# Spectral mixing and softmax attention on one core: the planner counts loaded matrix entries as usable later

## Chip, cores and metric

The kernel runs on one core of one Trainium2 chip. The metric is the device time of one execution in microseconds (us); lower is better. TensorE (PE) does the matrix products, ScalarE (ACT) the exponentials and copies, VectorE (DVE) and GpSimd (POOL) elementwise work, SyncE (SP) issues most of the transfers.

## Reference

Two branches over different inputs x [1, 2048, 448]; their results stand side by side in an output [1, 2048, 896].

```python
# A: spectral mixing, y = Re(DFT_seq(DFT_hidden(x))), with the DFT matrices given as inputs
a = einsum("bsd,ed->bse", x, dft_hid_re)
b = einsum("bsd,ed->bse", x, dft_hid_im)
y = einsum("ts,bse->bte", dft_seq_re, a) - einsum("ts,bse->bte", dft_seq_im, b)
# B: attention with 16 heads of 28
q, k, v = split((x @ wqkv))                 # wqkv [448, 3 * 448]
p = softmax(q @ k.T * 28 ** -0.5)           # 2048 x 2048 for each head
out = (p @ v) @ wo
concatenate([y, out], axis=-1)
```

The two sequence matrices are 2048 x 2048 f32, 16 MB each.

## The kernel before

**What is computed where.** The attention goes head by head. For one head, TensorE makes the scores of 16 key tiles by 4 query chunks of 512 (L1280), ScalarE takes their exponentials (L1286), and TensorE multiplies them by the values (L1263). Ahead of each head its first key tile is treated apart to get the shift of the exponentials: scores (L1221), a copy by ScalarE (L1225), transposes and maxima on VectorE (L1226 to L1247), a cast of the shift row into the queries (L1250), a subtraction from the first tile's scores (L1252, "the shift"; on VectorE or GpSimd), and the exponentials of this tile (L1254). A head ends with ScalarE's copy of the output bank (L1312), a reciprocal on VectorE (L1314 to L1320), a product on GpSimd (L1323) and stores to an intermediate tensor (L1329).

**The filling.** TensorE's remaining time goes to the projections (L684) and to the spectral branch (L864), which is stored through L1091, L1092, L1093 (sum and difference halves), L1117 and L1119 (output rows) and the transfers L1124 (GpSimd) and L1131 (SP). Behind the attention stands the output projection: loads of its operand (L1399, L1406, L1410), a split in high and low parts (L1424 on ScalarE, L454 elsewhere) and matmuls (L1444).

**The matrix check.** The sequence matrices are used in folded form. Beside the attention the kernel loads their entries into six raw buffers of 512 KB (`raw_s`, NRAW = 6) and looks at whether they have the symmetry that the folding takes for granted: differences and sums of two buffers (L950, on GpSimd 2.3 or VectorE 1.2 us in the plan) and the largest absolute value (L896, `far`). Most loads go through SP in ascending row order (L915). Entries that must be read in descending order (class `Turned`) go through GpSimd's own queue: four pieces of 128 KB (L938), and for some of them two edge loads (L943), which wait for all four pieces.

**What sets the order.** Nothing is ordered by hand. Each instruction is a task with a key (its due time, in planned us), the engines that may take it with a planned duration, and the tasks that it needs. `Schedule.run` plays the plan through: an idle engine takes the ready task with the smallest key, and a task becomes ready when its inputs count as there. The order in which the plan took them is the order in which each engine's queue is written; on the chip every engine works its queue strictly in that order. So a planned duration that is wrong makes no error, it only puts instructions in another order.

When a load through SP counts as usable is

```python
landed.append(max(at + 1.35 + size / 170 + extra + ..., flow + 1.1))   # size in KB
lat = max(landed[-len(t.dmas):]) - at + 0.1 + t.slack
```

with `slack = SLACK` on the loads of matrix entries, of the projection pieces and of the input rows. A load through GpSimd (`far_dma`) counts as usable a fixed number of us after its issue.

The due times of the attention are spread evenly from T_ATT to T_END, `P_H = (T_END - T_ATT) / H` for each head; those of the filling follow the points of PACE, of which the last is (all work, T_FILL). T_OUT belongs to the output projection.

Of the kernel before, what the change touches and what calls it, by code (L numbers as in the profile page):

```python
# [33 lines left out]
NKEPT = 16  # L34
NKEYS = 4
NFILL = 1
SLACK = 3.0
FILL_AT = 48.0, 75.0
N_WARM = 9
N_FIRST = 3  # L40
# [310 lines left out]
def tile_kernel(ctx, tc, xa, wre, wim, wd, xb, wqkv, wo, out):  # L351
# [53 lines left out]
    class Half:  # L405


        def __init__(self, pair, i):
            self.pair, self.i = pair, i
# [24 lines left out]
    def dma(key, emit, size=256, extra=0.0, n=1, **kw):  # L434

        return sch.add({"SP": 0.4}, key, lambda e: emit(), dmas=[(size, extra)] * n, **kw)

    def far_dma(key, emit, lat, d=1.2, **kw):

        return sch.add({"POOL": d}, key, lambda e: emit(), lat=lat, **kw)  # L440

    def act(key, emit, d=ACT_P, **kw):
        return sch.add({"ACT": d}, key, lambda e: emit(), **kw)
# [4 lines left out]
    def pool(key, emit, d=POOL_2, **kw):  # L448
        return sch.add({"POOL": d}, key, lambda e: emit(), **kw)
# [16 lines left out]
            nc.vector.tensor_copy(dst, src)  # L466


    T_ATT, T_END, T_FILL, T_OUT = 50.0, 620.0, 660.0, 630.0
    P_H = (T_END - T_ATT) / H  # L470
    begins = [T_ATT + h * P_H for h in range(H)]
    dt = P_H / (NT * NC)
# [9 lines left out]
    def fkey(n, d):  # L482

        f = clock[0]
        clock[0] += n * d
        for (f0, t0), (f1, t1) in zip(PACE, PACE[1:]):
            if f < f1 or f1 == F_TOTAL:
                return t0 + (f - f0) * (t1 - t0) / (f1 - f0)
# [87 lines left out]
    def load_folded(part, key, after):  # L576
# [3 lines left out]
        cols = slice(part * D, (part + 1) * D)  # L580
        lw = [dma(key, lambda: nc.sync.dma_start(w()[:, :, :E], wd[:, :2, part * D:part * D + E]), 226, slack=SLACK, use=[raws[2]])]
        ld = dma(key + 0.5, lambda: nc.sync.dma_start(n()[:, :, :D], wd[:, :2, cols]), 448, acq=[raws[0]])
        ld2 = dma(key + 0.7, lambda: nc.sync.dma_start(n2()[:, :, :D], wd[:, 2:, cols]), 448, acq=[raws[1]])
        ld3 = [dma(key + 1, lambda: nc.sync.dma_start(r()[:, :, :E], wt_d[:, :, part * D:part * D + E]), 226, slack=SLACK, deps=turned[0], use=[raws[3]])]
        f = lambda l: w_first.folded[:, part, :, l, :]
# [17 lines left out]
    class Piece:  # L603


        def __init__(self, src, key):
            self.hi, self.lo = whi.slot(), wlo.slot()
            raw = Square(raw_s.slot())
            ld = dma(key, lambda: nc.sync.dma_start(raw.t, src()), 256, slack=SLACK, acq=[raw])
            a = act(key + 1, lambda: nc.scalar.activation(self.hi.t, raw.t, AF.Copy), ACT_S, soon=SOON,  # L610
# [189 lines left out]
    def tokens(c, key, after):  # L800
# [6 lines left out]
        for q, st in enumerate((c, NH - 1 - c)):  # L807
            ln.append(dma(key + 0.3 * q, lambda q=q, st=st: nc.sync.dma_start(
                n.t[:, q].rearrange("p (b x) -> p b x", b=2), bass.AP(tensor=xa.tensor, offset=xa.offset + st * tile_x,
                ap=[[4 * P, P], [NH * tile_x, 2], [1, 2 * P]])), 256, slack=SLACK, use=[n]))  # L810
            lr.append(dma(key + 0.3 * q + 0.1, lambda q=q, st=st: nc.sync.dma_start(
                r.t[:, q].rearrange("p (b x) -> p b x", b=2), bass.AP(tensor=xt_d.tensor, offset=xt_d.offset + st * tile_x // 2,
                ap=[[2 * P, P], [NH * tile_x // 2, 2], [1, 2 * P]])), 256, slack=SLACK, deps=turned[1], use=[r]))
        z = [pool(key, lambda p=p, k=k: nc.gpsimd.memset(r.t.rearrange("p a (b k m) -> p (a b) k m", b=2, k=2)[p:p + 1, :, k], 0.0), 0.3, deps=lr, use=[r])
# [84 lines left out]
    row_n, tile_n = NT * P, P * NT * P  # L899
# [3 lines left out]
    def begun(key):  # L903
        return [opened[min(max(int((key - begins[0]) / P_H), 0), H - 1)]]

    class Stack:
# [6 lines left out]
        def loads(self, part, key, n, off, step):  # L913
            src, rows = (wre, wim)[part], P // n
            return [dma(key, lambda a=a: nc.sync.dma_start(self.t[a * rows:(a + 1) * rows], bass.AP(  # L915
                tensor=src.tensor, offset=src.offset + off(a), ap=[[step, rows], [1, H1]])), 512 / n, slack=SLACK, deps=begun(key), use=[self.raw]) for a in range(n)]

# [14 lines left out]
    class Turned(Stack):  # L932


        def __init__(self, part, b, key):
            self.raw = raw = raw_s.slot()
            src = (wre, wim)[part]
            at = lambda rows, cols, off, ap: far_dma(key, lambda: nc.gpsimd.dma_start(self.t[rows, cols], bass.AP(  # L938
                tensor=src.tensor, offset=src.offset + off, ap=[[tile_n, 4], *ap, [1, cols.stop - cols.start]])), 5.0 + SLACK, d=0.7, deps=begun(key), use=[raw])
            q = H1 // 4  # L940
            self.ld = [at(slice(0, P), slice(i * q, (i + 1) * q), H1 + i * q + (P - 32 * b) * row_n, [[-row_n, 32]]) for i in range(4)]
            if not b:
                at = lambda cols, off: far_dma(key, lambda: nc.gpsimd.dma_start(self.t[0:P:32, cols], bass.AP(  # L943
                    tensor=src.tensor, offset=src.offset + off, ap=[[tile_n, 4], [1, cols.stop - cols.start]])), 3.0 + SLACK, d=0.6, deps=self.ld[:4], use=[raw])
                self.ld += [at(slice(0, H1 - P), H1 + P), at(slice(H1 - P, H1), 0)]
# [409 lines left out]
    key = fkey(0, 0)  # L1355
# [35 lines left out]
    for n, c in enumerate(range(NC)):  # L1391
        raws = []
        for k in range(4):
            pair = kept_s.slot()
            raw = Half(pair, 0)
            key = T_OUT + n
            deps = [o_done[h, c] for h in range(H - 1) if (h + 1) * DH > k * P and h * DH < (k + 1) * P] + [before["k"] if n > 1 else opened[H - 1], *starts[max(4 * n - 8, 0):max(4 * n - 7, 0)]]
            if k < 3:
                ld = dma(key, lambda raw=raw, k=k, c=c: nc.sync.dma_start(raw.t, on_d[k * P:(k + 1) * P, c * CH:(c + 1) * CH]),  # L1399
                         deps=deps, use=[pair])  # L1400
# [13 lines left out]
        for i in range(2):  # L1414
            x = [Flat(p.slot()) for p in (whi, whi, wlo, wlo)] if i else [q_s.slot() for _ in range(4)]
            ready = [[], []]
            for k in range(4):
                raw, ld = raws[k]
                src = lambda raw=raw, i=i: raw.t[:, i * HF:(i + 1) * HF]
# [3 lines left out]
                key = T_OUT + T_CONV + n + i / 2  # L1423
# [3 lines left out]
                else:  # L1427
                    b = sub(key, lambda hi=hi: hi()[64:], lambda src=src: src()[64:], lambda hi=hi: f32(hi())[64:], d=0.35, early=True,
                            deps=[a], use=[raw.pair, xh, xl])
                ready[k // 3] += [a, b]  # L1430
            for t in range(2):
# [7 lines left out]
                key = T_OUT + O_AT + (n * 4 + i * 2 + t) * 2.3 + (100 if final else 0)  # L1439

                def emit(e, seq=seq, o=o, at=0, to=9):
                    for n, (x, w) in enumerate(seq):
                        if at <= n < to:
# [8 lines left out]
                             deps=[m], use=[o, pair]) for way, c0, c1 in ways]  # L1452
# [157 lines left out]
```

## Time and profile before

| what | value |
|---|---|
| time, median of 3 runs | 761.42 us (760.31 to 763.87) |
| profiled execution | 760.66 us, its span 759.1 us |
| TensorE busy | 719.0 us (95%), granted clock 0.979 |
| ScalarE busy | 610.1 us (80%) |
| VectorE busy | 532.7 us (70%) |
| GpSimd busy | 368.3 us (49%) |
| bytes moved | 127.80 MB, mean 168 GB/s |

The busy times are of one execution. Waits stand beside them in brackets: the idle time of an engine just before an instruction, and what ended it. The granted clock of TensorE is a share of its full speed, as a mean over the stretch asked for. From about 60 to 704 us the sixteen heads run one behind another; the copies L1312 mark their ends (the first at 108.00, the last at 704.34).

### The profile page before, as it was taken

To read this page: it belongs to the slowest core of one execution; us is meant where nothing else is said; L and a number is where in the kernel's file an instruction comes from. 1 tells how busy PE (TensorE), PEld (TensorE's weight loads), DVE (VectorE), ACT (ScalarE), POOL (GpSimd) and SP (SyncE) were. 2 spreads that over 40 slices of the span, in tenths; PEclk is the share of its full clock that TensorE was granted. 3 is DMA by queue.
4 is the path that set the end of the run, shared out by engine and by line. 5 is a ranking of instruction groups with operands and counts; after the bars stand their busy time and mean duration, and the time that the engine had idled before them with its cause. 6 is when DMAs were issued, how large, how long until landed. Compare 5 with 4: busy or idle time off the path is not lost. (4 is left out here: it accounts for less than half of the span.)

```text
span 759.1 us, 12950 instructions
## 1 busy us (share of the span) xinstructions
PE 719.0 (95%) x4147; PEld 402.8 (53%) x4147; DVE 532.7 (70%) x872; ACT 610.1 (80%) x1232; POOL 368.3 (49%) x357
## 2 busy tenths in 40 slices
PE   8899999989999997999799999899999999999877
PEld 7697444545545453454334454445445554555766
DVE  5558539767777889686687688987989846522752
ACT  6316899878989988899687999888989899999142
POOL 7202425655262656572545447555787433436640
PEclk9999999999999999999889999999999999999989
DMA  8657539674859989967678397657161413331466
GB/s 307 221 175 219 137 85 239 166 200 120 219 151 214 259 200 250 223 181 177 166 197 222 105 247 191 184 169 231 53 183 58 118 33 82 93 87 53 111 185 223
DMA packets 116160, 127.80 MB, mean 168 GB/s; under 512 B 54470, under 2 KB 80728, under 8 KB 116084
## 3 DMA queue, kind: packets, MB, share of 16 engines
q1 hardware_dynamic: 109300, 120.75, 58.2%
q0 software_dynamic: 6784, 6.14, 3.4%
q8 instruction: 35, 0.57, 0.3%
q14 instruction: 41, 0.34, 0.2%
HBM read 96.64 MB, written 32.69 MB: 170 GB/s over the span
## 5 line engine op out<-in xcount | busy, mean ns | idle before, releaser
L1286 ACT ACTIVATE kept<-bank 128x512 f32<-128x512 f32 x960 | 499.2, 687 | 38.8 <-PE bank L1280 36.9
L1280 PE MATMUL bank<-q,k 98*128 98x512 f32 x960 | 316.1, 423 | 17.5 <-ACT kept L1286 10.7
L1280 PEld LDWEIGHTS bank<-q,k 98*128 98x128 f32 x960 | 172.9, 190 | 173.7 <-issue 92.4
L1263 PE MATMUL bank<-kept,v 128*32 128x512 f32 x2048 | 248.9, 607 | 0.5 <-ACT kept L1286 0.5
L950 POOL TENSOR_TENSOR raw<-raw,raw 128x1024 f32<-128x1024 f32 (+3 forms) x60 | 119.9, 2003 | 107.4 <-DMA raw<-wre 55.2
L1263 PEld LDWEIGHTS bank<-kept,v 128*32 128x32 f32 x2048 | 55.8, 110 | 121.2 <-issue 114.2
L896 DVE TENSOR_REDUCE far<-raw 128x1 f32<-128x1024 f32 (+2 forms) x78 | 86.2, 1111 | 17.1 <-POOL raw L950 10.7
L1226 DVE STREAM_TRANSPOSE mb<-bank 128x512 f32<-128x512 f32 x64 | 45.3, 710 | 48.2 <-PE bank L1221 44.4
L1250 POOL CAST q<-mb 1x512 fp32r<-1x512 f32 x32 | 27.7, 870 | 67.5 <-DVE mb L1247 61.8
L1254 ACT ACTIVATE kept<-kept 128x512 f32<-128x512 f32 x64 | 46.8, 749 | 15.9 <-DVE kept L1252 11.4
L1225 ACT ACTIVATE kept<-bank 128x512 f32<-128x512 f32 x64 | 40.5, 673 | 22.4 <-PE bank L1221 18.6
L684 PE MATMUL bank<-big,whi 128*128 128x512 f32 x132 | 50.2, 409 | 7.1 <-DVE kept L707 4.4
L1323 POOL TENSOR_TENSOR kept<-kept 128x512 f32<-128x512 f32 x16 | 20.6, 1285 | 67.2 <-DVE kept L1318 36.6
L1252 POOL TENSOR_TENSOR kept<-kept,mb 128x512 f32<-128x512 f32 x32 | 43.6, 1368 | 11.1 <-DVE mb L1247 8.3
L1227 DVE TENSOR_REDUCE qm<-mb 128x16 f32<-128x512 f32 x64 | 43.3, 679 | 1.4
L1247 DVE STREAM_TRANSPOSE mb<-am 128x512 f32<-128x512 f32 x64 | 43.2, 695 | 0.8
L684 PE MATMUL bank<-wd,big 128*128 128x224 f32 x288 | 43.7, 278 | 0.0
L684 PEld LDWEIGHTS bank<-wd,big 128*128 128x128 f32 x288 | 40.5, 195 | 5.2 <-issue 2.5
L1314 DVE STREAM_TRANSPOSE kept<-kept 128x512 f32<-128x512 f32 x16 | 11.3, 708 | 39.3 <-ACT kept L1312 39.3
L1252 DVE TENSOR_TENSOR kept<-kept,mb 128x512 f32<-128x512 f32 x32 | 35.3, 1107 | 0.5
L950 DVE TENSOR_TENSOR raw<-raw,raw 128x1024 f32<-128x1024 f32 (+3 forms) x24 | 34.1, 1420 | 1.9 <-DMA raw<-wre 1.8
L1250 DVE CAST q<-mb 1x512 fp32r<-1x512 f32 x32 | 34.1, 1079 | 0.8
(174 smaller groups left out, 819.7 us busy)
## 6 DMA issues: line engine op xcount, KB each, us to landing
raw<-wre SPq DMA_DIRECT2D x64, 256.0 KB
raw<-wim SPq DMA_DIRECT2D x64, 256.0 KB
qkd<-kept SPq DMA_DIRECT2D x40, 256.0 KB
k<-qkd SPq DMA_DIRECT2D x64, 112.0 KB
q<-qkd SPq DMA_DIRECT2D x64, 112.0 KB
kept<-xb SPq DMA_DIRECT2D x16, 256.0 KB
vd<-kept SPq DMA_DIRECT2D x32, 128.0 KB
v<-vd SPq DMA_DIRECT2D x16, 256.0 KB
```

Source lines behind the costliest of these rows:

```text
L684: nc.tensor.matmul(o.t[:, :cols], w(), x(), start=(i == 0), stop=(i == n - 1))
L896: far_done.append(dve(key, lambda: nc.vector.tensor_reduce(far[rows, part, n:n + 1], t(), axis=AX.X if len(t().shape) == 2 else AX.XY, op= ...
L950: return sch.add(d, at, lambda g: eng[g].tensor_tensor(xv(), xv(), yv(), op=op), deps=[*x.ld, *y.ld, *deps], use=[x.raw, y.raw])
L1226: t = dve(key, lambda o=o, tm=tm: nc.vector.transpose(tm.t, o.t), 0.73, deps=[m], acq=[tm], use=[o], lock=[o], own=RAW_S)
L1227: rs.append(dve(key, lambda tm=tm, c=c: nc.vector.tensor_reduce(qm.t[:, 0, c * NT:(c + 1) * NT], tm.t.rearrange("p (j r) -> p j r", r=32), ...
L1247: t = dve(key, lambda mb=mb, c=c: nc.vector.transpose(mb.t, f32(am.t)[:, c * NT:(c + 1) * NT].unsqueeze(2).to_broadcast([P, NT, 32])), 0.7 ...
L1250: row.append(sch.add({"DVE": 0.7, "POOL": 0.7}, key, lambda e, q=q, mb=mb: eng[e].tensor_copy(q.t[96:97, :], mb.t[96:97, :]), deps=[t], us ...
L1252: sh = sch.add({"DVE": 0.92, "POOL": POOL_2}, key, lambda e, s=s, mb=mb: eng[e].tensor_tensor(s.t, s.t, mb.t, op=ALU.add), deps=[t, made[c ...
L1254: shown.append(act(key, lambda s=s: nc.scalar.activation(s.t, s.t, AF.Exp, scale=SCALE), ACT_S, deps=[sh], use=[s.pair]))
L1263: nc.tensor.matmul(o.t[c * VW:(c + 1) * VW, :], VT[h].t[:, kt // 4, kt % 4, :], tiles[c].t, start=(kt == 0), stop=(kt == NT - 1))
L1280: m = pe(key, lambda e, o=o, q=q, kt=kt: nc.tensor.matmul(o.t, KT[h][kt // 4].t[:KM, kt % 4 * P:(kt % 4 + 1) * P], q.t[:KM, :], start=True ...
L1286: es[h, kt].append(act(key - 20, lambda o=o, p=p: nc.scalar.activation(p.t, o.t, AF.Exp, scale=SCALE), deps=[m], use=[o, p.pair]))
```

## The change

Three numbers that the plan uses are changed; all instructions stay.

```diff
-SLACK = 3.0
+SLACK = 5.0
+T_FAR = 13.0
...
-    T_ATT, T_END, T_FILL, T_OUT = 50.0, 620.0, 660.0, 630.0
+    T_ATT, T_END, T_FILL, T_OUT = 50.0, 625.0, 655.0, 630.0
...
         def __init__(self, part, b, key):            # class Turned
...
             at = lambda rows, cols, off, ap: far_dma(key, lambda: nc.gpsimd.dma_start(self.t[rows, cols], bass.AP(
-                tensor=src.tensor, ..., ap=[[tile_n, 4], *ap, [1, cols.stop - cols.start]])), 5.0 + SLACK, d=0.7, deps=begun(key), use=[raw])
+                tensor=src.tensor, ..., ap=[[tile_n, 4], *ap, [1, cols.stop - cols.start]])), T_FAR, d=0.7, deps=begun(key), use=[raw])
```

A load of matrix entries through SP counts as usable 5 us past its planned landing instead of 3. A descending piece counts as usable 13 us past its issue instead of 5.0 + 3.0 = 8. The two edge loads of `Turned` keep their form 3.0 + SLACK and so go from 6 to 8. P_H goes from 35.625 to 35.9375, and the last point of the filling lies 5 us earlier. The lines of the changed kernel are one higher than before (L938 is L939).

The queues change in many places. Four pieces of them follow, first before, then after. The buffer numbers (raw_74, kept_100, mb_116) are dealt by the plan too and differ; mb holds a first tile's transposed shift, q and kept what the shift is applied to.

GpSimd's queue at the end of the second head and in the third, around the first descending pieces. Before:

```order
L1323 TENSOR_TENSOR kept_109<-kept_109 128x512
L938 DMA raw_74<-wre 128x1x256 x4
L943 DMA raw_74<-wre 4x896
L943 DMA raw_74<-wre 4x128
L978 COPY col_80<-raw_75 128x8
L950 TENSOR_TENSOR raw_71<-raw_71,raw_75 128x1024
L950 TENSOR_TENSOR raw_74<-raw_74,raw_73 128x8x128
L1250 CAST q_96<-mb_116 1x512
L1252 TENSOR_TENSOR kept_100<-kept_100,mb_116 128x512
L950 TENSOR_TENSOR raw_70<-raw_70,raw_73 128x512 x2
L1252 TENSOR_TENSOR kept_100<-kept_100,mb_117 128x512
```

After:

```order
L1324 TENSOR_TENSOR kept_101<-kept_101 128x512
L939 DMA raw_71<-wre 128x1x256 x4
L944 DMA raw_71<-wre 4x896
L944 DMA raw_71<-wre 4x128
L979 COPY col_80<-raw_70 128x8
L951 TENSOR_TENSOR raw_74<-raw_74,raw_70 128x1024
L1253 TENSOR_TENSOR kept_110<-kept_110,mb_116 128x512
L951 TENSOR_TENSOR raw_70<-raw_70,raw_72 128x8x127
```

The shift L1252 stood behind the edge loads, two L950 and a cast; now one L950 stands between the edge loads and it.

GpSimd's queue in the eighth head, around the descending pieces of the second matrix. Before:

```order
L1323 TENSOR_TENSOR kept_104<-kept_104 128x512
L950 TENSOR_TENSOR raw_73<-raw_73,raw_70 128x8
L938 DMA raw_73<-wim 128x1x256 x2
L950 TENSOR_TENSOR raw_71<-raw_71,raw_70 128x1024
L938 DMA raw_73<-wim 128x1x256 x2
L943 DMA raw_73<-wim 4x896
L950 TENSOR_TENSOR raw_74<-raw_74,raw_75 128x1024
L943 DMA raw_73<-wim 4x128
L950 TENSOR_TENSOR raw_75<-raw_75,raw_70 128x8x127
L950 TENSOR_TENSOR raw_75<-raw_75 128x8
L938 DMA raw_70<-wim 128x1x256
L1250 CAST q_94<-mb_116 1x512
```

After:

```order
L1324 TENSOR_TENSOR kept_110<-kept_110 128x512
L939 DMA raw_71<-wim 128x1x256 x4
L944 DMA raw_71<-wim 4x896
L944 DMA raw_71<-wim 4x128
L951 TENSOR_TENSOR raw_72<-raw_72,raw_70 128x1024
L1251 CAST q_92<-mb_116 1x512
L951 TENSOR_TENSOR raw_70<-raw_70,raw_75 128x8x127
L951 TENSOR_TENSOR raw_71<-raw_71,raw_74 128x8x128
L951 TENSOR_TENSOR raw_73<-raw_73,raw_74 128x512
L1251 CAST q_94<-mb_116 1x512
L1253 TENSOR_TENSOR kept_115<-kept_115,mb_116 128x512
L939 DMA raw_71<-wim 128x1x256
```

The four pieces were issued in two pairs behind two L950; now all four follow the product L1323 (now L1324) that closes a head, and a check's L950 no longer stands between the two edge loads.

VectorE's queue at the same place. Before:

```order
L1247 STREAM_TRANSPOSE mb_116<-am_121 128x512
L1247 STREAM_TRANSPOSE mb_117<-am_121 128x512
L1250 CAST q_92<-mb_116 1x512
L1252 TENSOR_TENSOR kept_103<-kept_103,mb_116 128x512
L896 TENSOR_REDUCE far<-raw_74 128x1
L1250 CAST q_93<-mb_117 1x512
L1252 TENSOR_TENSOR kept_103<-kept_103,mb_117 128x512
L1247 STREAM_TRANSPOSE mb_116<-am_121 128x512
L896 TENSOR_REDUCE far<-raw_75 128x1
```

After:

```order
L1248 STREAM_TRANSPOSE mb_116<-am_121 128x512
L1248 STREAM_TRANSPOSE mb_117<-am_121 128x512
L1253 TENSOR_TENSOR kept_111<-kept_111,mb_116 128x512
L897 TENSOR_REDUCE far<-raw_72 128x1
L1251 CAST q_93<-mb_117 1x512
L1253 TENSOR_TENSOR kept_111<-kept_111,mb_117 128x512
L951 TENSOR_TENSOR raw_70<-raw_70 128x8
L897 TENSOR_REDUCE far<-raw_70 128x1
L1248 STREAM_TRANSPOSE mb_116<-am_121 128x512
L897 TENSOR_REDUCE far<-raw_71 128x1
```

Between the first two shifts a check L896 (now L897) stands as before, and a cast L1250 has gone to GpSimd; ahead of the third transpose a second L950 and L896 (now L951 and L897) have come.

SP's queue at the end, from the stores of the spectral branch on. Before:

```order
L1131 DMA out<-kept_102 16x448
L1131 DMA out<-kept_102 15x448
L1131 DMA out<-kept_102 32x448 x3
L1131 DMA out<-kept_102 16x448
L1131 DMA out<-kept_102 15x448
L1131 DMA out<-kept_102 32x448 x3
L1410 DMA kept_113<-kept_110 28x512 x2
L1410 DMA kept_101<-kept_110 28x512 x2
L1131 DMA out<-kept_114 32x448 x8
L1131 DMA out<-kept_107 32x448 x8
L1399 DMA kept_108<-ond 128x512
L1399 DMA kept_103<-ond 128x512
```

After:

```order
L1132 DMA out<-kept_102 16x448
L1132 DMA out<-kept_102 15x448
L1132 DMA out<-kept_102 32x448 x3
L1132 DMA out<-kept_102 16x448
L1132 DMA out<-kept_102 15x448
L1132 DMA out<-kept_102 32x448 x3
L1132 DMA out<-kept_115 32x448 x8
L1411 DMA kept_108<-kept_112 28x512 x2
L1411 DMA kept_114<-kept_112 28x512 x2
L1132 DMA out<-kept_102 32x448 x8
L1132 DMA out<-kept_111 32x448 x6
L1400 DMA kept_106<-ond 128x512
```

Before, 26 stores L1131 and four L1410 stood ahead of the next loads L1399; now 32 stores and four.

More of the change, by code (lines that the diff above doesn't have):

```diff
@@ L938, in __init__ @@
             at = lambda rows, cols, off, ap: far_dma(key, lambda: nc.gpsimd.dma_start(self.t[rows, cols], bass.AP(
-                tensor=src.tensor, offset=src.offset + off, ap=[[tile_n, 4], *ap, [1, cols.stop - cols.start]])), 5.0 + SLACK, d=0.7, deps=begun(key), use=[raw])
+                tensor=src.tensor, offset=src.offset + off, ap=[[tile_n, 4], *ap, [1, cols.stop - cols.start]])), T_FAR, d=0.7, deps=begun(key), use=[raw])
             q = H1 // 4
```

## Prediction

> **What bounds the kernel now.** I read the busy shares, then stretches of one head each, then what ended TensorE's idle time, and last the queues of GpSimd and VectorE around the two largest of those gaps.
>
> ```profile
> PE 719.0 (95%) x4147; PEld 402.8 (53%) x4147; DVE 532.7 (70%) x872; ACT 610.1 (80%) x1232; POOL 368.3 (49%) x357
> core 0: us, PE busy (x) PEld busy (x) DVE busy (x) ACT busy (x) POOL busy (x), PEclk, DMA share, GB/s
> 142.50:185.50 43.00, 40.48 (x245) 21.94 (x241) 31.85 (x54) 34.83 (x70) 23.98 (x22) 0.92 0.59 155
> 306.00:343.00 37.00, 37.00 (x221) 18.75 (x217) 28.10 (x41) 35.30 (x72) 21.85 (x15) 1.00 0.73 197
> 343.00:388.50 45.50, 40.49 (x218) 19.50 (x210) 32.95 (x43) 35.87 (x73) 22.11 (x21) 0.92 0.71 177
> ```
>
> The first three stretches are one head each, from one head's output copy L1312 to the next (the third, seventh and eighth of sixteen). The undisturbed one (306 to 343) takes 37.0 us, and TensorE is busy in all of it. The stretch from 343 takes 45.5 us, although its 40.49 busy us at a clock of 0.92 are only 37.3 us of work at full clock; the one from 142.5 has 40.48 × 0.92 = 37.2 us of work in 43.0. ScalarE is busy for 35.30 of the 37.0 too. So the work of TensorE, with ScalarE close behind, bounds the attention; only the disturbances can be won, at most 45.5 − 37.3 = 8.2 and 43.0 − 37.2 = 5.8 us in these two.
>
> ```profile
> PE bank L1280 <- ACT kept L1286: 10.7, 10, 5.0
> PE bank L684 <- DVE kept L707: 4.4, 3, 2.9
> PE bank L1280 <- POOL q L1250: 2.2, 1, 2.2
> ```
>
> These are TensorE's largest waits between 60 and 705 us: total, times, longest. The 5.0, and one of 2.34, lie in the two long heads, where the first tile of the following head is prepared. The first, from the timelines of GpSimd, ScalarE and TensorE (start, duration, in brackets the idle time ahead and what ended it):
>
> ```profile
> 146.96 2.87 POOL L938 DMA_DIRECT2D raw<-wre  x4
> 159.19 1.10 POOL L943 DMA_DIRECT2D raw<-wre  x2 [9.37 <-DMA raw<-wre]
> ...
> 164.09 2.36 POOL L950 TENSOR_TENSOR raw<-raw,raw 128x1024 f32<-128x1024 f32 x1 [0.86 <-DMA raw<-wre]
> 166.51 1.48 POOL L1250 CAST q<-mb 1x512 fp32r<-1x512 f32 x1
> 168.07 1.28 POOL L1252 TENSOR_TENSOR kept<-kept,mb 128x512 f32<-128x512 f32 x1
> 169.39 0.63 ACT L1254 ACTIVATE kept<-kept 128x512 f32<-128x512 f32 x1 [4.24 <-POOL kept L1252]
> 167.88 2.50 PE L1280 MATMUL bank<-q,k 98*128 98x512 f32 x5 [2.34 <-DMA raw<-wre]
> ```
>
> GpSimd issues the four descending pieces, then stands 9.37 us before the edge loads (L943), because they wait for all four. The matrix work and a cast run before the shift L1252 of the next head's first tile. ScalarE reaches that tile's exponential at 165.15 and idles 4.24 us; its banks stay full and TensorE stops for 2.34 us (the releaser named there landed long before). The second is the same in another shape, with VectorE between:
>
> ```profile
> 345.41 1.30 POOL L1323 TENSOR_TENSOR kept<-kept 128x512 f32<-128x512 f32 x1 [4.75 <-DVE kept L1318]
> ...
> 356.41 1.38 POOL L938 DMA_DIRECT2D raw<-wim  x2 [3.32 <-DVE far L896]
> 360.13 1.37 POOL L938 DMA_DIRECT2D raw<-wim  x2
> 369.33 0.55 POOL L943 DMA_DIRECT2D raw<-wim  x1 [7.83 <-DMA raw<-wim]
> 369.90 2.40 POOL L950 TENSOR_TENSOR raw<-raw,raw 128x1024 f32<-128x1024 f32 x1
> 372.34 1.22 DVE L896 TENSOR_REDUCE far<-raw 128x1 f32<-128x1024 f32 x1 [6.60 <-POOL raw L950]
> 375.18 0.69 DVE L1252 TENSOR_TENSOR kept<-kept,mb 128x512 f32<-128x512 f32 x1
> 375.90 0.63 ACT L1254 ACTIVATE kept<-kept 128x512 f32<-128x512 f32 x1 [5.33 <-DVE kept L1252]
> 377.07 0.80 PE L1280 MATMUL bank<-q,k 98*128 98x512 f32 x1 [5.01 <-ACT kept L1286]
> ```
>
> Here VectorE stands 6.60 us before the check L896, which waits for GpSimd's L950 behind L943; the shift is two places further back in VectorE's queue. After each gap TensorE is slow:
>
> ```profile
> 166.00:170.00 4.00, 2.12 (x5) 1.49 (x5) 3.96 (x8) 0.61 (x2) 3.86 (x4) 0.68 0.54 162
> 170.00:174.00 4.00, 3.82 (x14) 2.39 (x17) 3.96 (x4) 3.99 (x10) 4.00 (x4) 0.50 0.47 144
> 376.00:380.00 4.00, 2.93 (x11) 1.23 (x15) 4.00 (x5) 4.00 (x9) 3.12 (x4) 0.50 0.73 186
> 380.00:384.00 4.00, 4.00 (x19) 1.56 (x11) 3.97 (x3) 1.98 (x5) 4.00 (x4) 0.69 0.67 178
> ```
>
> Work lost to the clock is busy × (1 − granted): 2.12 × 0.32 + 3.82 × 0.50 = 2.6 after the first gap, 2.93 × 0.50 + 4.00 × 0.31 = 2.7 after the second. A whole disturbance therefore costs 2.34 + 2.6 = 4.9 and 5.01 + 2.7 = 7.7 us.
>
> The Trainium skill (TensorE: Matmul & The Clock Gate, Part 1) says that the clock halves after an idle window of about 3.4 us. By it the first gap would cost 2.3 and the sum below would be 2.6 us smaller; the granted 0.50 behind a gap of 2.34 us disagrees, so the rows are used.
>
> **The change, part by part.** No instruction of work is added or taken away; queues are dealt anew.
>
> *13 us for the descending pieces.* The plan had 8 us; the rows show the last piece landing 9.37 and 7.83 us after the issues end, so the order put work directly behind L943 as if it were about to start. With 13, before the first gap one L950 (2.36, plus 0.86 waiting) and the cast (1.48) no longer stand ahead of the shift on GpSimd: it would start at 168.07 − 4.8 = 163.3 and end at 164.6, before 165.15. The wait of 9.37 us stays where it is, but ScalarE does not feel it. Value −4.9; bounds 0 and −5.8 (the head's surplus). I take −4.9: the margin of 0.55 us is small, but a shift that comes 1 us later still saves most of the 4.24. In the second head the four issues stand right behind L1323 (345.41 + 1.30), not from 356.41 and 360.13 on: they end near 349.6, land by about 349.6 + 7.8 = 357.4, and L943 and L950 (0.55 × 2 + 2.40) end at 361, some 11 us before 372.3. L896 then starts right behind the shift ahead of it, near 366, and the late shift (3.5 us behind L896's start, 375.18 + 0.69 − 372.34) ends at 369.5, before ScalarE comes to it at 375.90 − 5.33 = 370.6. Value −7.7; bounds 0 and −8.2.
>
> *5 instead of 3 us past landing for the matrix loads.* The plan adds SLACK to 1.35 us plus 256 KB at 170 KB per us, so 5.9 us before and 7.9 after.
>
> ```profile
> DMA to landing us min/median/max: 1.8/6.4/9.4
>   POOL raw L950: 91.8, 19
> ```
>
> These are from the view of the tile raw, loads and waiters: the median landing of 6.4 lies between the two plans, and GpSimd's L950 waited 19 times, 91.8 us in all, for SP's loads. GpSimd has slack (49% busy), so these waits matter only where a head's shift stands behind one. The other TensorE waits above and their slow clock are dealt anew without a direction that I can read: 0, bounds −12 and +12, since the other waits come to 10.7 − 5.0 + 4.4 + 2.2 = 12.3. One thing can be read: in the new order the seventh and the twelfth head have matrix work ahead of their transposes on VectorE that was not there before. I charge one new wait of the size of 2.2 (the POOL q L1250 row) with a part of a clock loss: +3; bounds 0 and +7.7.
>
> *Deadlines.* Heads come due 0.31 us later each, filling 5 us earlier at its end. Hence two chains of L864 (12 matmuls each) stand inside the attention that stood behind it, and the first 18 stores L1131 can be issued before the loads of the last projection batch become urgent.
>
> ```profile
> L1286 ACT ACTIVATE kept<-bank 128x512 f32<-128x512 f32 x960 | 499.2, 687 | 38.8 <-PE bank L1280 36.9
> 705.16 6.08 SPq L1131 DMA_DIRECT2D out<-kept  x10
> 711.34 4.26 SPq L1410 DMA_DIRECT2D kept<-kept  x4
> 715.71 11.87 SPq L1131 DMA_DIRECT2D out<-kept  x16
> 727.74 1.00 SPq L1399 DMA_DIRECT2D kept<-ond  x2
> 704.12 1.60 PE L864 MATMUL bank<-big 128*128 128x226 f32 x12
> 729.85 0.47 PE L1444 MATMUL bank<-wd,wlo 128*128 128x448 f32 x1 [2.74 <-POOLq L1477]
> 736.31 18.06 PE bank L1444 x85
> ```
>
> Before, SP issues 30 transfers back to back from 705.16, and the loads L1399 start only at 727.74, 23.6 us after the attention (704.12); TensorE's last 18.06 us stand behind them. Now 36 stand ahead, but the first ten follow a chain whose copy stands 18 exponentials before the attention's end in ScalarE's queue, 18 × 0.52 (499.2/960) = 9.4 us earlier; with the halves on VectorE and GpSimd behind it I put them at −9 to −3, the next eight at 0 to +5. At 0.61 us each (6.08/10), with four L1410 (4.26), and the last six waiting for their chain until about +14, L1399 starts near +19: −4.6. TensorE cannot follow quite: the two chains cost 24 × 1.60/12 = 3.2 us inside an attention that is full, and give it back behind, where they stood partly beside waits. I take −3; bounds +3.2 (chains paid, nothing won) and −4.6 − 2.74 = −7.3 (TensorE's own gap closes too).
>
> Sum: −4.9 − 7.7 + 0 + 3 − 3 = −12.6. The profiled execution took 760.66 (span 759.1); 760.66 − 12.6 = 748.1. The runs' median of 761.42 lies 0.76 higher, so I forecast 748.8.
>
> **The rivals.** (a) *The disturbances only move* (chance 0.17). If the matrix work ahead of the seventh and twelfth heads' transposes stalls as these did, 4.9 + 7.7 are paid again in place of the 3: 761.4 − 12.6 − 3 + 12.6 = 758.4, within 0.5% of before. For it: the loads still land when they land, and GpSimd's waits of 91.8 us must stand somewhere. Against: the order shows more distance behind every issue.
>
> (b) *Slots and SP's queue* (0.14), the slower side. A raw buffer is planned to be held 2 us longer (5 for a descending one), there are six, and SP issues in order: a matrix load that waits for a buffer holds the next head's k and q loads behind it, and TensorE stops at L1280. The trace before has no wait on k or q, so the nearest price is the 7.7 above. Two such heads eat the 15.6 us of gains, three give 761.4 − 15.6 + 23.1 = 769. Against it: the plan also delays the instructions that the buffers serve, and deals SP's issues with the same clock.
>
> (c) *The first two go, the end does not* (0.14): no gain in the queue of SP and 3.2 for the chains gives 761.4 − 12.6 + 3 + 3.2 = 755, faster all the same.
>
> (d) *The landing time was never the cause* (0.05): pieces that land soon make 13 for 8 worthless, only the end's −3 stays, 758.4.
> The Trainium skill (DMA: Bandwidth & Descriptors, Anatomy of one DMA — SWDGE (gpsimd) path) fits 2.0 us + bytes/436e3, some 2.3 us for a piece of 128 KB, which speaks for (d); the 9.37 and 7.83 us speak against it.
>
> The forecast itself holds 0.50, with 744 to 754 as its own range.
>
> **How the numbers follow.** About 0.5% (3.8 us) is what a measurement of this kernel can tell. Faster: the forecast, (c), and a fifth of (a): 0.50 + 0.14 + 0.03 = 0.67. Same: the rest of (a) and (d): 0.14 + 0.05 = 0.19. Slower: (b), 0.14. The range leaves out the worst half of (b) and the outcomes in which the re-dealt waits all fall well: 739 (748.8 less most of the 12 us) to 764.
>
> **What would show it.** Right: no wait of ScalarE over 2 us at L1254 (now L1255) in the third and eighth heads, lengths of 37 to 39 us for them, a granted clock of 0.95 or more there; L1399's second batch (now L1400) within 20 us of the last L1263 (now L1264). Wrong: a wait of TensorE of over 3 us while the seventh or twelfth head is prepared; a wait named k or q; the edge loads standing longer than 9.4 us.

## Result and profile after

The changed kernel takes 737.8 us (median of 4 runs, 736.5 to 742.1) against 762.0 for the kernel before: ratio 0.969, 95% interval 0.965 to 0.974. The forecast was 748.8 with a range from 739 to 764. The direction was right; the gain of 24 us is about twice the 12.6 forecast, and the time lies just below the range. The profiled execution has a span of 737.0 us (before 759.1). The attention's last output copy stands at 686.22 us (before 704.34), and 50.8 us follow it (before 54.8): of 22.1 us, 18.1 lie ahead of this copy and 4.0 behind it. Of the 18.1, 2.1 lie ahead of the first head's copy (108.00, now 105.88); they are not the change's, since x3 below, which works its queues in the order of the changed kernel, has this copy at 108.74. (The profiled execution of one experiment below, e3, was a disturbed one; of its times only the end explains anything here.)

The same heads as in the prediction, third, seventh and eighth, and the ninth, by windows from copy to copy (TensorE's busy time is the second number, its granted clock the third from the end):

```profile
core 0: us, PE busy (x) PEld busy (x) DVE busy (x) ACT busy (x) POOL busy (x), PEclk, DMA share, GB/s
141.02:181.90 40.88, 39.61 (x245) 21.65 (x248) 31.58 (x51) 35.75 (x72) 22.10 (x21) 0.96 0.62 164
298.99:336.97 37.98, 37.51 (x217) 18.46 (x220) 32.46 (x45) 35.48 (x74) 21.27 (x14) 1.00 0.91 231
336.97:375.23 38.26, 37.33 (x219) 19.64 (x212) 30.00 (x41) 36.25 (x74) 22.33 (x22) 1.00 0.67 180
375.23:412.47 37.24, 36.97 (x219) 18.47 (x221) 30.64 (x41) 35.79 (x73) 15.87 (x13) 1.00 0.84 212
```

The eighth head has gone from 45.4 to 38.3 us, at full clock. The third has gone from 43.0 to 40.9 and misses the predicted 37 to 39: its clock is 0.96, and TensorE still waits 1.3 us there, for another VectorE operation (L791). The ninth, of which the prediction said nothing, has gone from 43.3 to 37.2. Around the pieces of the third head GpSimd and ScalarE now read

```profile
145.29 2.87 POOL L939 DMA_DIRECT2D raw<-wre  x4
155.20 1.12 POOL L944 DMA_DIRECT2D raw<-wre  x2 [7.03 <-DMA raw<-wre]
...
157.03 2.39 POOL L951 TENSOR_TENSOR raw<-raw,raw 128x1024 f32<-128x1024 f32 x1 [0.51 <-DMA raw<-wre]
159.39 1.46 POOL L1253 TENSOR_TENSOR kept<-kept,mb 128x512 f32<-128x512 f32 x1
163.11 0.72 ACT L1255 ACTIVATE kept<-kept 128x512 f32<-128x512 f32 x1
```

GpSimd still stands 7.03 us before the edge loads, but the shift ends at 160.85 and ScalarE comes to it at 163.11 without waiting. In the eighth head (GpSimd's timeline):

```profile
339.62 1.30 POOL L1324 TENSOR_TENSOR kept<-kept 128x512 f32<-128x512 f32 x1 [2.39 <-DVE kept L1319]
340.86 2.71 POOL L939 DMA_DIRECT2D raw<-wim  x4
352.53 1.11 POOL L944 DMA_DIRECT2D raw<-wim  x2 [8.96 <-DMA raw<-wim]
```

The four pieces follow L1324 at once; before, they went 9.7 and 13.4 us behind the end of L1323. The wait before the edge loads is no shorter, only earlier against the head. What ScalarE waits for at the first tiles' exponentials, over the whole attention, sums these up ("shift waits" below). Before (total, times, longest):

```profile
ACT kept L1254 <- DVE kept L1252: 11.4, 6, 5.3
ACT kept L1254 <- POOL kept L1252: 4.5, 2, 4.2
```

After:

```profile
ACT kept L1255 <- POOL kept L1253: 0.8, 1, 0.8
```

And the end, by SP's timeline, TensorE's and the chain that ended last:

```profile
686.51 6.16 SPq L1132 DMA_DIRECT2D out<-kept  x8
692.77 4.62 SPq L1411 DMA_DIRECT2D kept<-kept  x4
697.50 9.99 SPq L1132 DMA_DIRECT2D out<-kept  x14
707.59 1.32 SPq L1400 DMA_DIRECT2D kept<-ond  x3
686.01 0.93 PE L865 MATMUL bank<-big 128*128 128x226 f32 x6
702.11 1.40 PE L1445 MATMUL bank<-wd,q 128*128 128x448 f32 x4 [2.96 <-DVE q L455]
719.33 12.49 PE bank L1445 x61
```

The first ten stores are gone from the stretch behind the attention; L1400 starts 21.6 us behind it (707.59 against 686.01, where L865 follows the last product; before 23.6 behind 704.12), and TensorE's last run is 12.49 us with 61 matmuls (before 18.06 with 85).

### The profile page after: what moved, and what is told of

Same layout as the page of the kernel before. It is cut to its first block, busy times and chain, and to the rows that moved or that the text cites. A ratio compares the mean times of both kernels' runs of the same rounds, so it can differ in the third digit from the quotient of the medians.

```text
span 737.0 us, 12989 instructions
## 1 busy us (share of the span) xinstructions
PE 706.6 (96%) x4147; PEld 399.0 (54%) x4147; DVE 524.6 (71%) x879; ACT 607.3 (82%) x1227; POOL 352.4 (48%) x355
## 4 chain that ended last, share of the span: by engine, by line
PE 69%; DVE 13%; ACT 5%; DMA 5%; issue 2%; POOL 2%; SPq 1%; DVEq 0%; ACTq 0%; POOLq 0%
PE bank L1281 25%; PE bank L1264 24%; PE bank L685 11%; ACT kept L1287 4%; PE bank L1445 2%; PE bank L727 2%; PE bank L865 2%; PE bank L1222 2%; DMA k<-qkd 1%; DVE kept L1253 1%; DVE mb L1248 1%; DMA raw<-wqkv 1%; DVE far L897 1%; DVE qm L1234 1%; DVE raw L951 1%
## 5 line engine op out<-in xcount | busy, mean ns | idle before, releaser
L1287 ACT ACTIVATE kept<-bank 128x512 f32<-128x512 f32 x960 | 500.9, 690 | 38.4 <-PE bank L1281 36.5
L1281 PE MATMUL bank<-q,k 98*128 98x512 f32 x960 | 310.9, 419 | 10.5 <-ACT kept L1287 4.4
L951 POOL TENSOR_TENSOR raw<-raw,raw 128x1024 f32<-128x1024 f32 (+3 forms) x48 | 95.1, 1988 | 83.6 <-DMA raw<-wre 40.7
L897 DVE TENSOR_REDUCE far<-raw 128x1 f32<-128x1024 f32 (+3 forms) x78 | 86.5, 1113 | 6.2 <-POOL raw L951 3.6
L1227 DVE STREAM_TRANSPOSE mb<-bank 128x512 f32<-128x512 f32 x64 | 44.9, 707 | 32.8 <-PE bank L1222 29.9
L1324 POOL TENSOR_TENSOR kept<-kept 128x512 f32<-128x512 f32 x16 | 20.6, 1290 | 85.9 <-DVE kept L1319 43.1
L1253 POOL TENSOR_TENSOR kept<-kept,mb 128x512 f32<-128x512 f32 x38 | 53.2, 1408 | 13.1 <-DVE mb L1248 9.3
L951 DVE TENSOR_TENSOR raw<-raw,raw 128x1024 f32<-128x1024 f32 (+2 forms) x36 | 46.0, 1279 | 0.5 <-DMA raw<-wim 0.3
L1253 DVE TENSOR_TENSOR kept<-kept,mb 128x512 f32<-128x512 f32 x26 | 30.8, 1191 | 0.2
L685 PEld LDWEIGHTS bank<-big,whi 128*128 128x128 f32 x132 | 24.7, 189 | 9.7 <-DVE big L455 2.6
```

The lines of the kernel that those rows point to most:

```text
L685: nc.tensor.matmul(o.t[:, :cols], w(), x(), start=(i == 0), stop=(i == n - 1))
L897: far_done.append(dve(key, lambda: nc.vector.tensor_reduce(far[rows, part, n:n + 1], t(), axis=AX.X if len(t().shape) == 2 else AX.XY, op= ...
L951: return sch.add(d, at, lambda g: eng[g].tensor_tensor(xv(), xv(), yv(), op=op), deps=[*x.ld, *y.ld, *deps], use=[x.raw, y.raw])
L1227: t = dve(key, lambda o=o, tm=tm: nc.vector.transpose(tm.t, o.t), 0.73, deps=[m], acq=[tm], use=[o], lock=[o], own=RAW_S)
L1253: sh = sch.add({"DVE": 0.92, "POOL": POOL_2}, key, lambda e, s=s, mb=mb: eng[e].tensor_tensor(s.t, s.t, mb.t, op=ALU.add), deps=[t, made[c ...
L1281: m = pe(key, lambda e, o=o, q=q, kt=kt: nc.tensor.matmul(o.t, KT[h][kt // 4].t[:KM, kt % 4 * P:(kt % 4 + 1) * P], q.t[:KM, :], start=True ...
```

## Experiments

In the table, shift waits are ScalarE's waits at the first tiles' exponentials, idle is TensorE's idle time between 60 us and the last output copy, end is the span behind that copy; these three are from one profiled execution each. Such a reading is not exact: e4 keeps the order of the kernel before, without the edge loads, and its sixth head takes 46.8 us instead of 43.4. The ratio is against the kernel before, timed on the same chip.

| kernel | SLACK | pieces | T_END, T_FILL | ratio (95%) | shift waits | idle | end |
|---|---|---|---|---|---|---|---|
| before | 3 | 8 | 620, 660 | 1 | 15.9 | 24.0 | 54.8 |
| e1 | 3 | 13 | 620, 660 | 1.001 (0.998 to 1.004) | 20.2 | 30.1 | 55.5 |
| e4 | 3, no edge loads | 8 | 620, 660 | 0.997 (0.994 to 0.9995) | 11.4 | 22.0 | 56.3 |
| e7 | 3 | 8 | 620.4, 660 | 1.003 (0.999 to 1.007) | 25.1 | 29.9 | 58.8 |
| e8 | 3 | 8 | 619.6, 660 | 0.996 (0.993 to 1.000) | 18.5 | 26.1 | 58.8 |
| e3 | 3 | 8 | 625, 655 | 0.991 (0.987 to 0.995) | 4.4 | 25.6 | 50.3 |
| e2 | 5 | 8 | 620, 660 | 0.987 (0.982 to 0.992) | 10.8 | 19.4 | 57.9 |
| e5 | 5 | 13 | 620, 660 | 0.990 (0.983 to 0.997) | 13.1 | 27.7 | 57.2 |
| x4 | 5, checks 2.5 early | 8 | 620, 660 | 0.993 (0.990 to 0.996) | 4.1 | 27.2 | 55.7 |
| e9 | 5 | 8 | 620, 655 | 0.984 (0.977 to 0.990) | 8.4 | 22.5 | 49.7 |
| e10 | 5 | 8 | 625, 660 | 0.980 (0.975 to 0.985) | 8.7 | 22.7 | 50.3 |
| e6 | 5 | 8 | 625, 655 | 0.966 (0.961 to 0.972) | 0.3 | 11.8 | 51.3 |
| after | 5 | 13 | 625, 655 | 0.969 (0.965 to 0.974) | 0.8 | 16.4 | 50.8 |
| x3 | 5, no edge loads | 13 | 625, 655 | 0.965 (0.958 to 0.972) | 0.8 | 15.8 | 49.9 |
| e11 | 5 | 13 | 625.4, 655 | 0.982 (0.978 to 0.986) | 3.9 | 23.8 | 49.6 |
| e12 | 5 | 13 | 624.6, 655 | 0.976 (0.972 to 0.981) | 2.7 | 20.0 | 49.4 |
| x2 | 4 | 13 | 625, 655 | 1.007 (1.003 to 1.010) | 10.7 | 30.7 | 50.2 |
| x1 | 7 | 13 | 625, 655 | 0.983 (0.977 to 0.989) | 1.4 | 24.5 | 49.7 |

**The three parts alone, and the wait itself.**

```diff
 e1:  -... 5.0 + SLACK, d=0.7 ...
      +... 13.0, d=0.7 ...
```

> The kernel before with the descending pieces counted as usable 13 us past their issue instead of 8, and nothing else changed. Theory L (planned landing times): both long heads that stood behind the edge loads lose their wait, 4.9 + 7.7 us, so about 749 against 761.5, with no ScalarE wait over 2 us ahead of the first tiles of the fourth and ninth heads. Theory R (re-dealing: any small shift of the plan's numbers deals the waits anew, and parts do not add): anything between 735 and 770, and other heads change by 5 us or more than those two.

Measured: no change, 1.001, so theory L is wrong. The third head takes 41.2 us, and the eighth became the longest of all, 51.2 us. GpSimd's and TensorE's timelines there:

```profile
345.46 1.29 POOL L1323 TENSOR_TENSOR kept<-kept 128x512 f32<-128x512 f32 x1 [4.33 <-DVE kept L1318]
351.73 0.22 POOL L950 TENSOR_TENSOR raw<-raw,raw 128x8 f32<-128x8 f32 x1 [4.99 <-DMA raw<-wim]
354.97 2.72 POOL L938 DMA_DIRECT2D raw<-wim  x4 [3.02 <-DVE far L896]
367.16 1.10 POOL L943 DMA_DIRECT2D raw<-wim  x2 [9.47 <-DMA raw<-wim]
...
376.43 0.79 PE L1280 MATMUL bank<-q,k 98*128 98x512 f32 x1 [5.04 <-ACT kept L1286]
388.63 0.80 PE L1280 MATMUL bank<-q,k 98*128 98x512 f32 x1 [4.85 <-ACT kept L1286]
```

The pieces are issued together, as in the changed kernel, yet 8 us behind L1323: a check waits for a load of matrix entries (4.99), and GpSimd waits another 3.02 us for L896, the last reader of the raw buffer. What lets the pieces start here is this chain, and not their own landing time.

```diff
 e2:  -SLACK = 3.0
      +SLACK = 5.0        # pieces kept at 8.0
```

> The kernel before with SLACK 5 instead of 3, the descending pieces kept at 8. Theory L: GpSimd's wait of 91.8 us for SP's loads shrinks, and of TensorE's waits outside the two long heads (12 us with as much lost to the clock) about half goes: 750 to 755. Theory R: 735 to 770, without relation to GpSimd's wait for loads.

Measured: 0.987, 754.3 us, within theory L's range. GpSimd's waits for SP's loads shrink from 91.8 to 80.9 us, TensorE's idle time falls by 4.6 and ScalarE's shift waits by 5, but the end is 3 us longer. The eighth head keeps a wait of TensorE of 3.8 us.

```diff
 e3:  -T_ATT, T_END, T_FILL, T_OUT = 50.0, 620.0, 660.0, 630.0
      +T_ATT, T_END, T_FILL, T_OUT = 50.0, 625.0, 655.0, 630.0
```

> The kernel before with T_END 625 and T_FILL 655 alone. Theory L: the two long heads stay long (43 and 45 us), only the end behind the attention gets shorter by about 4 us: 757. Theory R: 735 to 770, with the long heads at other places.

Measured: 0.991 (0.987 to 0.995), and an end of 50.3 us. That is 4.5 of the 6.8 us, as theory L said; the ten runs spread from 751 to 765 us, so that the ratio is less sure than its interval says. Something else in this run was not expected. In the eighth head GpSimd's queue has

```profile
353.96 1.28 POOL L1323 TENSOR_TENSOR kept<-kept 128x512 f32<-128x512 f32 x1 [7.01 <-ACT kept L1286]
355.20 2.71 POOL L938 DMA_DIRECT2D raw<-wim  x4
```

The deadlines alone, with SLACK 3 and 8 us for the pieces, put the four pieces right behind L1323.

The parts give 1.001, 0.987 and 0.991 alone, and 0.969 together, where their product is 0.979. That they help one another is not shown: the two neighbours e11 and e12 below, at 0.982 and 0.976, lie on either side of the product.

```diff
 e4:  -at = lambda cols, off: far_dma(key, lambda: nc.gpsimd.dma_start(...), 3.0 + SLACK, d=0.6, ...)
      +at = lambda cols, off: far_dma(key, lambda: None, 3.0 + SLACK, d=0.6, ...)
      -SAME = 2.0 ** -36
      +SAME = 2.0 ** 36
```

> The kernel before in its own order, instruction by instruction, without the four edge loads L943 for which GpSimd waits until all descending pieces have landed (the edge rows hold other entries, and the bound of the symmetry comparison is set so wide that they do not count). Theory L: in the eighth head GpSimd's check does not wait 7.83 us any more, and the 7.7 us of that head go; in the third head the next operation waits for loads of SP that land at 160.8 anyway, so that its 4.9 us stay: 761.5 - 7.7 = 753.8. If the waits at the edge loads are not what made that head long, the time stays within 2 us of before.

Measured: 0.997 (0.994 to 0.9995), some 2.5 us instead of 7.7; the eighth head is 2.3 us shorter. The wait of 7.83 us is gone, and this is what came instead (GpSimd, VectorE, ScalarE, TensorE; line numbers are one lower in e4 and x3 than in the kernel before and after):

```profile
362.32 4.49 POOL L949 TENSOR_TENSOR raw<-raw,raw 128x1024 f32<-128x1024 f32 x2
...
362.30 2.50 DVE L1235 CAST am<-am 32x64 fp32r<-32x64 f32 x1
364.83 2.01 DVE L977 COPY col<-raw 128x8 f32<-128x8 f32 x1
...
370.74 0.63 ACT L1253 ACTIVATE kept<-kept 128x512 f32<-128x512 f32 x1 [3.82 <-DVE kept L1251]
371.91 0.50 PE L1279 MATMUL bank<-q,k 98*128 98x512 f32 x1 [3.47 <-ACT kept L1285]
```

In the kernel before, the same two instructions of VectorE ran while GpSimd waited:

```profile
361.49 0.18 DVE L1236 CAST am<-am 32x64 fp32r<-32x64 f32 x1
361.70 0.17 DVE L978 COPY col<-raw 128x8 f32<-128x8 f32 x1
```

GpSimd's checks, freed from their wait, now run beside VectorE's preparation of the head, and two instructions of 0.18 and 0.17 us take 2.50 and 2.01. So the wait at the edge loads was part of what made the head long, but without it TensorE still stops for 3.47 us there, where it stopped for 5.01.

**Combinations, and what a change that means nothing is worth.**

```diff
 e5:  SLACK = 5.0, pieces 13.0, T_END 620.0, T_FILL 660.0
 e6:  SLACK = 5.0, pieces  8.0, T_END 625.0, T_FILL 655.0
 e7:  SLACK = 3.0, pieces  8.0, T_END 620.4, T_FILL 660.0
 e8:  SLACK = 3.0, pieces  8.0, T_END 619.6, T_FILL 660.0
```

> The kernel after without its new deadlines (T_END 620, T_FILL 660): SLACK 5 and 13 us for the pieces. Theory L, amended by the first four runs: 5 us for SP's loads is what frees the raw buffer early, so that the pieces of the eighth head can be issued right behind the product that ends a head, and only then do the 13 us keep the work behind the edge loads away from the shifts: eighth head 38 us, attention's end near 688, end part 55 us, 743 in all. Theory R (re-dealing): 735 to 770, no better than either alone.

Measured: 0.990; the eighth head takes 43.9 us, and its pieces go 8.6 us behind L1323. The amended theory L is wrong for this pair.

> The kernel after with the descending pieces put back to 8 us. Theory L as amended: third and eighth heads keep a wait (42 to 44 us each), the end part is 50 us as in the kernel after: 746 to 748. Theory R: 735 to 770. If it is as fast as the kernel after (738), the 13 us give nothing beside the other two.

Measured: 0.966: without the 13 us it is as fast as the kernel after. Its eighth head takes 37.2 us and its third 41.0; GpSimd's timeline in the eighth:

```profile
343.43 1.29 POOL L1323 TENSOR_TENSOR kept<-kept 128x512 f32<-128x512 f32 x1 [1.97 <-ACT kept L1286]
344.66 2.71 POOL L938 DMA_DIRECT2D raw<-wim  x4
355.14 1.09 POOL L943 DMA_DIRECT2D raw<-wim  x2 [7.76 <-DMA raw<-wim]
```

The pieces stand right behind L1323 with 8 in the plan too. So the 13 us are worth nothing that these runs can tell, neither alone (e1 against before), nor with SLACK (e5 against e2), nor with both (after against e6). What puts the pieces there is T_END. With 625 or 625.4 they follow the product at once, whatever the pieces' number and with SLACK 3, 4 or 5 (after, e3, e6, e10, e11, x2, x3), and 2.3 us later with SLACK 7 (x1); with 624.6 two go ahead of the product and two right behind it (e12); with 619.6 to 620.4 they follow it 8 us or more later (before, e1, e2, e4, e5, e7, e8, e9), but for x4, whose checks come due earlier.

> The kernel before with T_END 620.4 in place of 620.0, which means nothing: heads come due 0.025 us later each. It measures what a mere re-dealing is worth. Theory L: within 4 us of before (the same waits at the same heads). Theory R: 5 us or more away, to either side.

> The kernel before with T_END 619.6: a second draw of a shift that means nothing. Theory L: within 4 us of before. Theory R: 5 us or more away, to either side, and not to the same as with 620.4.

Measured: 1.003 and 0.996. A shift without meaning moves this kernel by 2 to 3 us, as theory L said, though the waits change: the eighth head takes 49.4 and 47.5 us. Shift waits are 25.1 and 18.5 us: with SLACK 3 and the old deadlines they are high in all four dealings (15.9 to 25.1).

**Which deadline, and how lucky the changed kernel is.**

```diff
 e9:   SLACK = 5.0, pieces  8.0, T_END 620.0, T_FILL 655.0
 e10:  SLACK = 5.0, pieces  8.0, T_END 625.0, T_FILL 660.0
 e11:  SLACK = 5.0, pieces 13.0, T_END 625.4, T_FILL 655.0
 e12:  SLACK = 5.0, pieces 13.0, T_END 624.6, T_FILL 655.0
```

> SLACK 5 with T_FILL 655, the attention's end kept at 620, the pieces at 8 us. Open is which of the two deadlines works with SLACK: SLACK and both gave 0.966, more than 0.987 times 0.991. If the filling's deadline brings the short end part (51 us against 55 to 58) and the attention's the rest: about 750, shift waits of ScalarE as with SLACK alone (some 10 us), end part 51 us.

> SLACK 5 with T_END 625, the filling's deadline kept at 660, the pieces at 8 us. If the attention's deadline moves the shifts ahead of the checks (the heads' tasks and the checks are ordered by one key): no waits of ScalarE for shifts, an end part of 55 us as before: about 746. If it does nothing by itself, as SLACK alone: 753.

Measured: 0.984 and 0.980. The first came out as expected. The second did not: either deadline alone shortens the end to about 50 us, and neither takes the shift waits away (8.4 and 8.7). The eighth head takes 38.5 and 38.4 us in the two, although its pieces go 8.2 us behind L1323 in e9 and at once in e10; so their early issue is one way to a short head and not the only one.

> The kernel after with T_END 625.4 in place of 625.0, which means nothing. If the gain rests on the numbers (later landing times, deadlines): 735 to 742. If it is one lucky dealing among many (theory R): 745 or more.

> The kernel after with T_END 624.6, a second draw around it. Numbers: 735 to 742. Theory R: 745 or more.

Measured: 0.982 and 0.976, which is 748 and 744 us where the kernel before takes 762 (on the chip of these runs it took 766.5, and they 751.2 and 747.9). Both keep more than half of the gain, and both miss the 735 to 742 that would have meant numbers alone. By these two, 5 to 10 of the changed kernel's 24 us belong to its own dealing. e6 speaks the other way: if the 13 us are worth nothing, it is a third neighbour, and it is as fast as the changed kernel. Four dealings of SLACK 5 with both deadlines thus lie between 0.966 and 0.982.

**How far SLACK goes.**

```diff
 x1:  SLACK = 7.0     x2:  SLACK = 4.0     # otherwise the kernel after
 x3:  the kernel after without its edge loads, as e4
 x4:  e2 with CHECK_AT, CHECK_STEP = 72.5, 90.0
```

> The kernel after with SLACK 7 in place of 5. If ScalarE's waits for shifts follow SLACK: they stay under 4 us, time 735 to 750 like the kernel after and its neighbours. If more slack only holds buffers longer: checks fall behind, 750 to 760.

> The kernel after with SLACK 4. If the waits follow SLACK: waits for shifts of 4 to 8 us, between SLACK 5 (0.8 to 4) and SLACK 3 with these deadlines (4.4), time 748 to 756. If all of it is re-dealing: no relation.

Measured: 0.983 and 1.007. With 4 neither number came as expected: the shift waits are 10.7 us, and at 767.8 us the whole gain is gone, although the end is short (50.2) and the eighth head's pieces follow L1324 at once; that head takes 45.4 us. With the new deadlines the shift waits are 4.4 us at SLACK 3 (e3), 10.7 at 4, 0.3 to 3.9 at 5 and 1.4 at 7. So they do not simply follow SLACK, and why 4 is so slow stays open. With 7 they stay under 4 us as expected, but the time of 752.1 us is the one expected of the other case: TensorE has other waits there, the largest group being

```profile
PE bank L1222 <- DMA q<-qkd: 5.2, 3, 2.8
```

These are the q loads, which are among TensorE's waits neither in the kernel before nor in the kernel after: the sign of rival (b). That buffers held longer cause them is not shown, since e3 with SLACK 3 has 3.2 us of them, and x3, in the order of the kernel after, 2.9.

> The kernel after in its own order without the edge loads (their rows then hold other entries, and the bound of the comparison is set so wide that they do not count). GpSimd stands 16 us before them. If 13 us in the plan have hidden that wait: no change, within 2 us of the kernel after, some 738. If it still costs: 2 to 5 us faster.

Measured: 0.965 (0.958 to 0.972), 739.1 us, no change against the kernel after. The 16 us that GpSimd stands before the edge loads there (7.03 + 8.96) are hidden; that e6 is as fast says that it is not the 13 that hides them.

> SLACK 5, pieces at 8 us, the deadlines of before, and the checks due 2.5 us earlier (CHECK_AT 72.5), about what T_END 625 gives on the average of the heads. If the attention's deadline works by bringing checks earlier against heads: waits for shifts of 8 us as with T_END 625, but an end part of 55 to 58 us, so 751 to 756. If it works otherwise: waits of 11 us or more as with SLACK 5 alone.

Measured: 0.993. The shift waits fall to 4.1, as bringing the checks forward should make them, but the sixth head alone takes 54.2 us, with TensorE waiting 5.3 us for casts of the shift row (L1250, on GpSimd) and 3.9 for q and k loads, at a clock of 0.87. The four pieces of the eighth head stand right behind L1323, as with T_END 625, and yet that head takes 44.3 us. So in this run checks that come due earlier against the heads do to the queue what T_END 625 does. That T_END works on the time by this alone is not shown.

## Why the prediction was right or wrong

*The bound and the places: right.* The prediction read two long heads out of windows and waits and priced them with the clock that they cost. Both waits for the shift are gone. The eighth head is 7.2 us shorter (forecast 7.7), the third only 2.1 (forecast 4.9). Of the signs named ahead, the short waits of ScalarE, the length of the eighth head and both clocks came; the length of the third head and L1400 within 20 us did not; none of the three signs of being wrong came.

*The step that failed first: the attribution of −4.9 and −7.7 to the 13 us.* The prediction saw GpSimd wait 9.37 and 7.83 us for pieces planned at 8, and took the number that names those pieces for the cause. e1 and e6 show the opposite: 13 alone gives 1.001, all without it 0.966. The trace before could have said so. For the descending pieces, from issue to landing, it has

```profile
DMA to landing us min/median/max: 3.6/6.8/9.4
```

So the planned 8 was short by 1.4 us at the worst, and the edge loads, which need all four pieces, stood 8 us behind them in the plan already. The early issue in the eighth head, which the prediction read rightly from the order, comes with T_END (e3, e10) and not with the 13. It does not by itself make the head short (x2, x4), so what brought the 7.2 us is known by its number and not by its whole chain. Since all was changed at once, the eighth head came out near its forecast by another cause, which is luck.

*A row that was read wrongly.* The prediction took 1.8/6.4/9.4 us for the landing of SP's loads and set it beside their plan of 5.9 and 7.9. It belongs to the 36 loads that GpSimd issues itself, the 32 pieces above and the four edge loads. No view here has the landing time of a load through SP. What the prediction had for these loads is GpSimd's 91.8 us of waits, and not a landing that is late against the plan.

*The mis-sized term: "0" for the re-dealt waits and "+3" for new ones.* The heads other than the first, third and eighth together became 6.7 us shorter, where +3 was forecast. In these are the ninth (−6.1), the fourth and twelfth (−3.0 and −3.2), and a slower thirteenth (37.4 to 43.0). In the seventh and twelfth, where new waits were expected, TensorE waits 0.5 us and not at all. Part of this could have been read: all shift waits together were 15.9 us, and the prediction priced only the two long ones. Part could not: the meaningless neighbours e11 and e12 lie 5 to 10 us from the changed kernel. That the forecast's ratio, 748.8/761.4 = 0.983, lies beside that of e11 is luck too, since its two largest terms had the wrong cause.

*The end: −3 forecast, −4.0 measured.* Ten profiles with either new deadline have an end of 49.4 to 51.3 us, eight without 54.8 to 58.8, so this term is the deadlines' and does not depend on the dealing. Its working was less exact than its sum. One chain of 12 matmuls moved inside the attention and not two: 44 of L864 stood behind it, 32 (now L865) stand there now. And L1400 came 21.6 us behind the attention and not 19: the 22 stores ahead of it took 0.73 us each (6.16 + 9.99 over 22) where 0.61 was charged.

*The clock: the rows were the right ones.* The granted clock over the eighth head, where the gap of 5.01 us was, is now 1.00. The work lost to the clock in the attention, busy × (1 − granted) by heads with the granted clock in hundredths, falls from 11.5 to 4.8 us, nearly as much as TensorE's idle time does (24.0 to 16.4).

*Rival (a)* did not come about. *(b)* has its sign, waits for q, in some of the experiments and not in the kernel after. *(c)* is out, since the end got shorter. *(d)* was nearest to the mechanism, with a chance of 0.05: 13 for 8 is worthless, as it says. Its result of 758.4 was wrong, since it gave SLACK and the deadlines nothing but the end.

## To carry to other kernels

Where a planner deals queues, a wait is named by its last releaser, and the number that plans this releaser need not be what moves it: follow the chain back to what was issued late, and set the planned landing beside the measured one (8 against 3.6 to 9.4) before changing it. Sum one kind of wait over the whole kernel before pricing its two longest cases. And measure a neighbour or two with a number shifted by nothing: here such shifts moved the kernel before by 2 to 3 us and the changed kernel by 5 to 10, and only what they all share (the shorter end, fewer shift waits) is the change's.

## What the hardware showed

A VectorE cast of 32x64 took 0.18 us while GpSimd waited, and 2.50 us while GpSimd ran L949 on raw buffers; a copy of 128x8 took 0.17 and 2.01. The longer copy ends at 366.84, GpSimd's second L949 at 366.81. The Trainium skill (SBUF — State Buffer, SBUF: two separate sides) says that a VectorE instruction in a two-port mode needs a port pair that GpSimd uses too, and that the one that starts first holds the pair for its whole instruction while the other is blocked. The times of e4 agree with it, though no row shows in which mode the cast and the copy ran. The delay is 4.2 us in VectorE's queue, ahead of the shift, and is one reason why taking GpSimd's wait of 7.83 us away shortened its head by 2.3 us only.
